# One 128x128 transpose for both heads' last 64 keys, with head 1's tail taken from its first 64 keys

## The chip, the core and the metric

The kernel runs on one core of a Trainium2 chip. The time is that of one execution on the device in microseconds (us), from three runs. A trace of one profiled execution gives the start and duration of the instructions of each engine: PE (TensorE matmuls; PEld is its weight load), DVE (VectorE), ACT (ScalarE), POOL (GpSimd) and SP (SyncE, which here only starts DMAs).

## The reference

Three blocks are chained; `B, H, S, D = 4, 8, 576, 64`, so the model width is 512.

```python
scores = scale * np.matmul(q, k.transpose(0, 1, 3, 2))
thresh = np.max(scores, axis=-1, keepdims=True) - tau
scores = np.where(scores >= thresh, scores, -1000000000.0)
attn = softmax(scores)                       # written out in the reference
x = (attn @ v) laid out as [B, S, H * D]
u = x + np.real(fft(fft(x, axis=1), axis=2))
un = (u - mean) / sqrt(var + 1e-06)
x = u + np.maximum(un @ w_ch1, 0.0) @ w_ch2
gate = sigmoid(causal convolution of x with conv_w, 5 taps)
out = (gate * (x @ w_val)) @ w_out
```

## The kernel before

The program order of each engine is written by hand. Attention runs over 16 pairs of heads (four pairs make one batch `b`). A pair has 576 queries a head, cut into nine tiles of 128 rows: for each of four blocks of 128 queries one tile for head 0 and one for head 1 (`h` = 0, 1), and one tile `h == 2` with the last 64 queries of both heads. That makes 144 tiles, two in each step of the loop `for u in range(NT // 2 + 3)`.

A tile goes through these stages, which the atoms of the string `ORDER` place within a step: S, the scores (PE, L573, into one of two PSUM score buffers); M, the row maximum (DVE, L585); E, the exponential (ACT, L592); K, the mask that multiplies the exponential with the comparison, writes the row tile `p` and sums the row (DVE, L602), and by that frees the score buffer; R and N, the reciprocal (DVE, L699) and the multiplication by it (POOL, L609, "the norm"); T, four 128x128 transposes of the probabilities, four tiles later (PE, L643); U, their copy from PSUM to SBUF (ACT, L652). S of the next tiles follows K of these.

A row tile `p` is [128, 1152]: head 0's 576 probabilities of 128 queries beside head 1's. Of the 576 keys, 512 (`MAIN`) go through the T transposes. The remaining 64 (`TAIL`, the last 64 of each head) are transposed by the tail work `g_tail` (L618 to L630): the transposes at L623 have 64 columns each and give a 64x128 result, ACT copies them to `th` (L628), and the product with `v` (`g_pv`, L302 to L325) ends with a fifth term that uses `th` against the tail rows `vt` of `v`, the lower 64 partitions of both being zero. There are four `p` buffers for five row blocks of a pair; the mask that starts on a buffer waits until the tail transposes of the block that held it are done.

PE's other work (tails, the transposes of q and k, the Fourier matmuls at L242, the products with v at L318) waits in queues. At P1 and P2 of each step `fill` draws from them up to a budget of estimated nanoseconds (1250 and 1350); each tail transpose counts 121.0, a product with v `n * 2 / 2.4`. Evacuations of finished fill work stand on ACT before the exponentials of the step (atom F1) or behind them (F2). `advance_side` (atom A) carries out the folds, the loads of v (`load_v`) and the addition of the FFT halves on DVE, POOL and SP. Conversions of the MLP's weights (WD, WP, WA; DVE L96 to L102, POOL L106) are spread over the steps. Behind attention `mlp` interleaves its first chunk with the Fourier work of batch 3 and then runs the MLP, the gate and the output.

Of the kernel before, what the change touches and what calls it, by code (L numbers as in the profile page):

```python
# [11 lines left out]
F32 = mybir.dt.float32  # L12
# [3 lines left out]
AF = mybir.ActivationFunctionType  # L16
ALU = mybir.AluOpType
# [4 lines left out]
B, H, S, D = 4, 8, 576, 64  # L22
# [4 lines left out]
MAIN, TAIL = 512, 64  # L27
# [107 lines left out]
def attention_fft(tc, right, ps_f, a, u_d, dram, conv_w, hooks):  # L135
    nc = tc.nc
    PE, DVE, ACT, POOL, SP = nc.tensor, nc.vector, nc.scalar, nc.gpsimd, nc.sync
    left, right1 = ExitStack(), ExitStack()
    with ExitStack() as right2, ExitStack() as right2b, ExitStack() as right3, ExitStack() as right4, ExitStack() as scores, ExitStack() as turned:
        def pool(stack, name, bufs, side="right", **kw):  # L140
            return stack.enter_context(tc.tile_pool(name=name, bufs=bufs, side=side, **kw))
# [3 lines left out]
        const = pool(right1, "const", 1)  # L145
# [13 lines left out]
        ident = id_p.tile([128, 128], F32, name="ident")  # L159
# [7 lines left out]
        ACT.activation(atau, alpha, AF.Exp)  # L167

        vs = [(const.tile([128, 2, 4, D], F32, name=f"v{i}"), const.tile([128, 2, D], F32, name=f"vt{i}")) for i in range(2)]
        ths = [[const.tile([128, 2, n], F32, name=f"th{i}_{n}") for n in (256, 320)] for i in range(2)]  # L170
        for t in [vt for _, vt in vs] + ths[0] + ths[1]:
            DVE.memset(t[64:128], 0.0)
        aeh = dft.tile([128, 3, CE], F32R, name="aeh")
        ael = dft.tile([128, 3, CE], F32R, name="ael")

# [33 lines left out]
        def load_v(p):  # L209
            b, hs = p // NP, slice(2 * (p % NP), 2 * (p % NP) + 2)  # L210
            v, vt = vs[p % 2]
            for h in range(2):
                SP.dma_start(out=v[:, h], in_=a["v"][b, hs, 0:MAIN][h].rearrange("(t p) d -> p t d", p=128))
            SP.dma_start(out=vt[0:64], in_=a["v"][b, hs, MAIN:S].rearrange("h p d -> p h d"))

        def g_consts():
            for nm, shape in (("cd", [128, 4, CE]), ("sd", [128, 4, DM // 2]), ("cs", [97, 3, KE]), ("ss", [96, 3, KE])):
# [14 lines left out]
        def fill_tile():  # L232
            state["open"] += 1
            return ps_f.tile([128, 512], F32, tag="f", name="f")

        def done(first, *then):

            evacs.append((first, then))
            state["put"] += 1
# [47 lines left out]
        def g_prep_v(p):  # L287
            while p >= 2 and (p - 2, 1) not in pv_done:
                yield
            load_v(p)  # L290
            vready.add(p)
# [3 lines left out]
        def x_tile(p):  # L295
            if p not in xt:
                xt[p] = x_p.tile([128, S], F32, tag="xt", name="xt")
            return xt[p]
# [3 lines left out]
        def g_pv(p, c):  # L302

            yield lambda: p in vready and tails.get((p, c), 0) == 1 + c and (p < XB or p - XB in folded)
            v, vt = vs[p % 2]
            x = x_tile(p)
            m, th = pt[p, c], ths[p % 2][c]
            yield "room"
            f = fill_tile()
            n = 256 if c == 0 else 320  # L310
            for t in range(5):
                for h in range(2):
                    w = v[:, h, t] if t < 4 else vt[:, h]
                    if t == 4:
                        r = th[:, h]
                    else:
                        r = m[:, h, t] if c == 0 else m[:, t, h * 320:h * 320 + 320]
                    PE.matmul(out=f[h * 64:h * 64 + 64, 0:n], lhsT=w, rhs=r, start=(t == 0), stop=(t == 4))  # L318
                    yield n * 2 / 2.4

            done(lambda: ACT.activation(x[:, c * 256:c * 256 + n], f[:, 0:n], AF.Copy))
            pv_done.add((p, c))
            if c == 1:
                yield "sync"
                side.append(g_fold(p))  # L325
# [5 lines left out]
        def g_fold(p):  # L331
            b, j = p // NP, p % NP
            x = xt.pop(p)
            while p and p - 1 not in folded or b and b - 1 not in spent_fold:
                yield
            if j == 0:
                fold[b] = [[fft_p.tile([128, NP, KE], F32R, tag=f"x{k}{i}", name=f"x{k}{i}") for i in "hl"] for k in "eo"]
                xs_d[b] = dram.tile([DM, S], F32, name=f"xs{b}")
            xs = xs_d[b]
            SP.dma_start(out=xs[j * 128:(j + 1) * 128], in_=x)  # L340
            xf = [None, None]
            w = (slice(0, HALF + 1), slice(1, HALF))

            def sums(kind):
                t = xf[kind] = tmp_p.tile([128, KE], F32, tag="xf", name="xf")
                POOL.tensor_tensor(out=t[:, 1:HALF], in0=x[:, 1:HALF], in1=x[:, S - 1:HALF:-1], op=ALU.subtract if kind else ALU.add)
                if kind == 0:
                    POOL.tensor_copy(t[:, 0:HALF + 1:HALF], x[:, 0:HALF + 1:HALF])  # L348

            def high_part(kind):  # L350
                ACT.activation(fold[b][kind][0][:, j, w[kind]], xf[kind][:, w[kind]], AF.Copy)

            def low_part(kind):
                h, l = (t[:, j, w[kind]] for t in fold[b][kind])
                POOL.tensor_tensor(out=l, in0=xf[kind][:, w[kind]], in1=f32(h), op=ALU.subtract)

            sums(0)
            yield
            sums(1)
            high_part(0)  # L360
            yield
            high_part(1)
            low_part(0)
            yield
            low_part(1)
            folded.add(p)
# [116 lines left out]
        q_prep, q_tail, q_pv, q_fft, q_mean = deque(), deque(), deque(), deque(), deque()  # L483
# [71 lines left out]
        p_t = {}  # L555

        def force(ready):
            while not ready():
                flush()
                advance_side()  # L560
                fill(1.0)
# [13 lines left out]

        def p_view(g):
            p, h, i = tiles[g]
            return p_t[p, i][:, h % 2 * S:h % 2 * S + S]

        def emit_max(g):  # L580
            if g % 2 == 0:
# [23 lines left out]
        def emit_norm(g):  # L605
            su = ssum[g // 2][:, g % 2:g % 2 + 1]
            v = p_view(g)
            p, h, i = tiles[g]
            POOL.tensor_scalar(out=v, in0=v, scalar1=su, scalar2=1.0, op0=ALU.mult, op1=ALU.mult)  # L609

        tq = []

        def pt_tile(p, c):
            if (p, c) not in pt:
                pt[p, c] = (pt0_p, pt1_p)[c].tile([128, 2, 4, 256] if c == 0 else [128, 4, 640], F32, tag=f"m{c}", name=f"m{c}")
            return pt[p, c]

        def g_tail(p, c, srcs, dst, rows):  # L618

            yield "room"  # L620
            f = fill_tile()
            for j, src in enumerate(srcs):
                PE.transpose(f[0:64, j * 128:(j + 1) * 128], src, ident)  # L623
                yield 121.0
            tailed.update((p, i) for i in rows)

            def first():
                ACT.activation(dst, f[0:64, 0:128 * len(srcs)].rearrange("k (h q) -> k h q", h=2), AF.Copy)  # L628
                tails[p, c] = tails.get((p, c), 0) + 1
            done(first)  # L630

# [2 lines left out]
        def emit_t(g):  # L634
            p, h, i = tiles[g]
            c = 0 if i < 2 else 1
            if (p, c) not in pt:
                force(lambda: p < 2 or (p - 2, c) in pv_done)
            m, th = pt_tile(p, c), ths[p % 2][c]
            f = ps_t.tile([128, 4, 128], F32, tag="t", name="t")  # L640
            pv = p_view(g)
            for t in range(4):
                PE.matmul(out=f[:, t, :], lhsT=pv[:, t * 128:(t + 1) * 128], rhs=ident, is_transpose=True, start=(t == 0), stop=(t == 3))  # L643
            if h == 2:
                o = m.rearrange("k t (h q) -> k t h q", h=2)[:, :, :, 256:320]
                fv = f.rearrange("k t (h q) -> k t h q", h=2)
            elif c == 0:
                o, fv = m[:, h, :, i * 128:(i + 1) * 128], f
            else:
                j = h * 320 + (i - 2) * 128  # L650
                o, fv = m[:, :, j:j + 128], f
            tq.append(lambda: ACT.activation(o, fv, AF.Copy))  # L652
            if h == 1 and i % 2 == 1:
                q_tail.append(g_tail(p, c, [p_t[p, i - 1 + j][:, hh * S + MAIN:hh * S + S] for hh in range(2) for j in range(2)], th[0:64, :, 0:256], (i - 1, i)))
            if h == 2:
                q_tail.append(g_tail(p, c, [p_t[p, i][:, MAIN:S]], th[0:64, :, 256:320], (i,)))

        LAG = 4
        SP.dma_start(out=ident, in_=a["ident"])
# [3 lines left out]
        for t in negs:  # L663
            for j in range(2):
                DVE.tensor_copy(t[:, j, 1:2], atau)
        DVE.tensor_scalar(out=alpha, in0=tau, scalar1=0.0, scalar2=float(D) ** -0.5,
                          op0=ALU.is_ge, op1=ALU.mult)
# [15 lines left out]
        for u in range(NT // 2 + 3):  # L683
            t = 2 * u
            on = [x for x in (t, t + 1) if x < NT]
            state["tile"] = t
            for x in on:
                p, h, i = tiles[x]
# [21 lines left out]
            def N0():  # L710
                if 0 <= t - 2 < NT: emit_norm(t - 2)
            def N1():
                if 0 <= t - 2 < NT: emit_norm(t - 1)
# [830 lines left out]
```

## Time and profile before

| what | value |
| --- | --- |
| times of three runs, us | 938.41, 938.17, 937.34 (median 938.17) |
| span of the profiled execution, first to last instruction, us | 936.0 (the page gives no other time of it) |
| busy share of PE, DVE, ACT, POOL | 94%, 59%, 48%, 39% |
| mean granted TensorE clock | 0.994 of full speed |
| steps of attention | from the start to about 395 us |
| one batch of attention (four pairs, 18 steps) | 96.5 us |

The busy shares are means over stages with different limits: the MLP keeps PE full, attention runs a loop over PE, DVE and ACT. What the change is worth has to be read in attention, where its instructions are, and at the places where other work waits for them.

### The profile page before, as it was taken

How to read it: one execution, taken by the hardware profiler on the slowest of the kernel's cores; microseconds unless marked ns; L12 is line 12 of the kernel's file. 1: busy time of each engine (PE TensorE's matmuls, PEld its weight loads, DVE VectorE, ACT ScalarE, POOL GpSimd, SP SyncE). 2: the span in 40 equal slices, each digit the busy share in tenths (PEclk: the TensorE clock that was granted, in tenths of full speed). 3: DMA queues.
4: the chain of work that ended last, by engine and by line, in shares of the span. 5: the costliest groups of instructions: out<-in, count | busy, mean ns of one | idle time of the engine just before them, and what ended most of it. 6: DMA issues, size and time to landing. Idle time of an engine off the chain costs nothing. (4 is left out here: it accounts for less than half of the span.)

```text
span 936.0 us, 14888 instructions
## 1 busy us (share of the span) xinstructions
PE 884.3 (94%) x5232; PEld 708.0 (76%) x5232; DVE 553.5 (59%) x1240; ACT 451.2 (48%) x915; POOL 368.0 (39%) x451
## 2 busy tenths in 40 slices
PE   6988899999999999799988999999999999999998
PEld 4555576657665765488866999999999989998897
DVE  5888888888887767316577243442412275735750
ACT  3778777777777766526355123213211313224432
POOL 2465645584467545612553321312111011037421
PEclk9999999999999999999999999999999999999999
DMA  6775545556555732587259524212110050233111
GB/s 151 190 193 129 165 119 167 154 163 173 164 142 172 193 92 72 178 314 234 89 204 351 204 91 130 79 46 85 52 66 1 1 178 3 91 130 122 70 46 68
DMA packets 135283, 123.34 MB, mean 132 GB/s; under 512 B 85686, under 2 KB 99238, under 8 KB 135208
## 3 DMA queue, kind: packets, MB, share of 16 engines
q1 hardware_dynamic: 126760, 97.57, 33.7%
q0 software_dynamic: 6960, 24.49, 8.5%
q8 instruction: 42, 0.69, 0.3%
q10 hardware_dynamic: 1488, 0.33, 0.2%
q14 instruction: 33, 0.27, 0.1%
HBM read 89.85 MB, written 37.22 MB: 136 GB/s over the span
## 5 line engine op out<-in xcount | busy, mean ns | idle before, releaser
L1072 DVE SCALAR_TENSOR_TENSOR hl<-h,hh 128x448 fp32r<-128x448 f32 (+1 forms) x80 | 51.0, 637 | 209.6 <-ACT hh L1071 209.6
L1071 ACT ACTIVATE hh<-h 128x448 fp32r<-128x448 f32 (+1 forms) x80 | 44.4, 555 | 262.9 <-PE h L1068 262.9
L609 POOL TENSOR_SCALAR p<-p,su 128x576 f32<-128x576 f32 x144 | 109.9, 769 | 91.1 <-DVE su L699 71.5
L602 DVE SCALAR_TENSOR_TENSOR p<-s,thr,e 128x576 f32<-128x576 f32 x144 | 112.6, 815 | 39.8 <-ACT e L592 21.9
L573 PE MATMUL s<-kt,qt 64*128 64x288 f32 (+1 forms) x640 | 101.3, 448 | 24.8 <-DVE p L602 24.8
L1084 PE MATMUL c<-hl,w1h 128*128 128x448 f32 (+1 forms) x320 | 118.9, 371 | 0.5 <-DVE hl L1072 0.5
L1084 PE MATMUL c<-hh,w1h 128*128 128x448 f32 (+1 forms) x320 | 118.8, 371 | 0.0
L1084 PE MATMUL c<-hh,w1l 128*128 128x448 f32 (+1 forms) x320 | 118.7, 371 | 0.0
L592 ACT ACTIVATE e<-s,neg 128x576 f32<-128x576 f32 x144 | 99.4, 737 | 28.5 <-DVE neg L585 27.9
L585 DVE TENSOR_REDUCE neg<-s 128x1 f32<-128x576 f32 x144 | 101.6, 745 | 14.5 <-PE s L573 14.5
L573 PEld LDWEIGHTS s<-kt,qt 64*128 64x128 f32 (+1 forms) x640 | 46.2, 178 | 66.3 <-issue 24.3
L652 ACT ACTIVATE m<-t 128x512 f32<-128x512 f32 x144 | 84.6, 588 | 6.5 <-PE t L643 6.4
L1068 PE MATMUL h<-unh,w0l 128*128 128x448 f32 (+1 forms) x320 | 81.9, 378 | 5.9 <-POOL w0l L106 5.9
L1068 PE MATMUL h<-unh,w0h 128*128 128x448 f32 (+1 forms) x320 | 80.5, 373 | 3.6 <-DMA w0h<-e_h 3.2
L318 PE MATMUL f<-m,v 128*64 128x320 f32 (+1 forms) x512 | 80.4, 415 | 1.5 <-ACT m L652 1.2
L1068 PE MATMUL h<-unl,w0h 128*128 128x448 f32 (+1 forms) x320 | 81.2, 376 | 0.0
L643 PE MATMUL t<-ident,p 128*128 128x128 f32 x576 | 77.9, 278 | 2.9 <-POOL xf L348 1.9
L643 PEld LDWEIGHTS t<-ident,p 128*128 128x128 f32 x576 | 64.3, 142 | 18.4 <-issue 10.3
L1068 PEld LDWEIGHTS h<-unh,w0l 128*128 128x128 f32 x320 | 60.8, 191 | 14.0 <-POOL w0l L106 7.2
L1068 PEld LDWEIGHTS h<-unh,w0h 128*128 128x128 f32 x320 | 59.9, 188 | 11.8 <-DMA w0h<-e_h 3.7
L1068 PEld LDWEIGHTS h<-unl,w0h 128*128 128x128 f32 x320 | 61.2, 191 | 7.2
L1084 PEld LDWEIGHTS c<-hl,w1h 128*128 128x128 f32 x320 | 60.1, 188 | 7.7 <-DVE hl L1072 0.9
(219 smaller groups left out, 1538.7 us busy)
## 6 DMA issues: line engine op xcount, KB each, us to landing
raw<-in_moe_w_ch POOLq DMA_DIRECT2D x32, 512.0 KB, 4.9
qn<-in_q SPq DMA_DIRECT2D x60, 128.0 KB, 2.9
xs<-xt SPq DMA_DIRECT2D x16, 288.0 KB, 4.1
e_h<-cx SPq DMA_DIRECT2D x18, 256.0 KB, 4.1
e_l<-ct SPq DMA_DIRECT2D x18, 256.0 KB, 5.3
w0h<-e_h SPq DMA_DIRECT2D x18, 256.0 KB, 6.7
w0l<-e_l SPq DMA_DIRECT2D x18, 256.0 KB
w1h<-e_h SPq DMA_DIRECT2D x18, 256.0 KB, 5.3
```

The source lines that it names most:

```text
L318: PE.matmul(out=f[h * 64:h * 64 + 64, 0:n], lhsT=w, rhs=r, start=(t == 0), stop=(t == 4))
L573: PE.matmul(out=s[o, c, 0:HALF], lhsT=qt[w, hh, q], rhs=kt[w, hh, :], start=True, stop=True)
L585: DVE.tensor_reduce(out=neg[i][:, j, 0:1], in_=sc[g][:, :, 0:HALF], axis=AX.XY, op=ALU.max, negate=True)
L592: ACT.activation(e, sc[g][:, :, 0:HALF], AF.Exp, bias=neg[g // 2][:, g % 2, 0:1], scale=1.0)
L602: DVE.scalar_tensor_tensor(out=p_view(g).rearrange("p (a b) -> p a b", a=2), in0=sc.pop(g)[:, :, 0:HALF], scalar=thr[g // 2][:, j], in1=ex ...
L609: POOL.tensor_scalar(out=v, in0=v, scalar1=su, scalar2=1.0, op0=ALU.mult, op1=ALU.mult)
L643: PE.matmul(out=f[:, t, :], lhsT=pv[:, t * 128:(t + 1) * 128], rhs=ident, is_transpose=True, start=(t == 0), stop=(t == 3))
L652: tq.append(lambda: ACT.activation(o, fv, AF.Copy))
L1068: PE.matmul(out=f[:, 0:n], lhsT=ww[:, k * 128:(k + 1) * 128], rhs=x[:, k, 0:n], start=(i == 0), stop=(i == 3 * KB - 1))
L1071: ACT.activation(hh, f[:, 0:n], AF.Relu)
L1072: DVE.scalar_tensor_tensor(out=hl, in0=f[:, 0:n], scalar=0.0, in1=f32(hh), op0=ALU.max, op1=ALU.subtract)
L1084: PE.matmul(out=ch[c][o][:, 0:n], lhsT=ww[:, o * 128:(o + 1) * 128], rhs=x, start=(at_ == 0 and i == 0), stop=(at_ == FB - 1 and i == 2))
```

## The change

Head 1's tail becomes its first 64 keys in place of its last 64. In a row of `p` head 0's last 64 columns (512 to 576) and head 1's first 64 (576 to 640) are neighbours, so one 128x128 transpose serves both heads. A pair then has five tail transposes of 128 columns (two for the first two row blocks, two for the next two, one for the tile `h == 2`) where it had nine of 64 columns; in all 80 and 144. `th` loses its head dimension; the zeros that keep the heads apart are now in `vt` alone, whose half for the other head is zero. The loads of v start 64 keys later for head 1, and the 64 rows for each head's `vt` come in two DMAs instead of one. In the tile `h == 2` both heads' queries share the columns of one mask, so the norm, which also puts them where the transposes expect them, becomes three POOL operations instead of one.

```diff
-        ths = [[const.tile([128, 2, n], F32, name=f"th{i}_{n}") for n in (256, 320)] for i in range(2)]
-        for t in [vt for _, vt in vs] + ths[0] + ths[1]:
-            DVE.memset(t[64:128], 0.0)
+        ths = [[const.tile([128, n], F32, name=f"th{i}_{n}") for n in (256, 320)] for i in range(2)]
+        for _, vt in vs:
+            for h in range(2):
+                DVE.memset(vt[64 - h * 64:128 - h * 64, h], 0.0)
...
             for h in range(2):
-                SP.dma_start(out=v[:, h], in_=a["v"][b, hs, 0:MAIN][h].rearrange("(t p) d -> p t d", p=128))
-            SP.dma_start(out=vt[0:64], in_=a["v"][b, hs, MAIN:S].rearrange("h p d -> p h d"))
+                src, o = a["v"][b, hs][h], h * TAIL
+                SP.dma_start(out=v[:, h], in_=src[o:o + MAIN].rearrange("(t p) d -> p t d", p=128))
+                o = (1 - h) * MAIN
+                SP.dma_start(out=vt[h * 64:h * 64 + 64, h], in_=src[o:o + TAIL])
...
                     if t == 4:
-                        r = th[:, h]
+                        r = th[:, 0:n]
...
-        return p_t[p, i][:, h % 2 * S:h % 2 * S + S]
+        return p_t[p, i][:, S if h else 0:S + S if h else S]
...
-            POOL.tensor_scalar(out=v, in0=v, scalar1=su, scalar2=1.0, op0=ALU.mult, op1=ALU.mult)
+            if h < 2:
+                parts = [(slice(0, 128), v, v)]
+            else:
+                rows = p_t[p, i]
+                parts = [(slice(0, 64), rows[:, 0:S], v), (slice(64, 128), rows[:, S:S + TAIL], v[:, 0:TAIL]),
+                         (slice(64, 128), rows[:, 0:MAIN], v[:, TAIL:S])]
+            for w, dst, src in parts:
+                POOL.tensor_scalar(out=dst[w], in0=src[w], scalar1=su[w], scalar2=1.0, op0=ALU.mult, op1=ALU.mult)
...
-            for j, src in enumerate(srcs):
-                PE.transpose(f[0:64, j * 128:(j + 1) * 128], src, ident)
+            th = ths[p % 2][c]
+            for j, i in enumerate(rows):
+                PE.transpose(f[:, j * 128:(j + 1) * 128], p_t[p, i][:, MAIN:MAIN + 2 * TAIL], ident)
                 yield 121.0
...
-                ACT.activation(dst, f[0:64, 0:128 * len(srcs)].rearrange("k (h q) -> k h q", h=2), AF.Copy)
+                if len(rows) == 2:
+                    ACT.activation(th[:, 0:256], f[:, 0:256], AF.Copy)
+                else:
+                    for h in range(2):
+                        w = slice(h * 64, h * 64 + 64)
+                        ACT.activation(th[w, 256:320], f[w, w], AF.Copy)
...
-            pv = p_view(g)
+            pv = p_t[p, i][:, S + TAIL:] if h == 1 else p_t[p, i][:, 0:MAIN]
```

The budgets of `fill` are as before, and so is the estimate of 121.0 for a tail transpose: with fewer of them, other work is drawn earlier, and the order on PE changes from the first batch's Fourier work on. From the first MLP matmul on it is the same again.

PE in the third batch of attention, before: the stretch from one pair of S (first two rows) to the next (the last row); `s<-kt,qt` are the scores, `t<-ident,p` the T transposes, `f<-ident,p` tails, `f<-m` and `f<-th` products with v, `f<-ssl,boh` Fourier matmuls.

```order
L573 MATMUL s<-kt,qt 128x288 x2
L573 MATMUL s<-kt,qt 64x288 x4
L242 MATMUL f<-ssl,boh 128x290 x3
L318 MATMUL f<-m_3332,v_197 64x256 x5
L643 MATMUL t<-ident,p 128x128 x8
L318 MATMUL f<-m_3332,v_197 64x256 x3
L318 MATMUL f<-th_256_201,vt_198 64x256 x2
L623 MATMUL f<-ident,p 64x128 x4
L318 MATMUL f<-m_3449,v_197 64x320
L573 MATMUL s<-kt,qt 128x288 x4
```

After, the stretch between the same two pairs of S (line numbers are those of the changed kernel):

```order
L576 MATMUL s<-kt,qt 128x288 x2
L576 MATMUL s<-kt,qt 64x288 x4
L245 MATMUL f<-csh,ael 128x290 x2
L245 MATMUL f<-csl,aeh 128x290 x3
L245 MATMUL f<-ssh,boh 128x290 x3
L245 MATMUL f<-ssh,bol 128x290 x3
L659 MATMUL t<-ident,p 128x128 x8
L245 MATMUL f<-ssl,boh 128x290 x3
L634 MATMUL f<-ident,p 128x128 x2
L576 MATMUL s<-kt,qt 128x288 x4
```

The product with v that stood on both sides of T has gone to other stretches, Fourier matmuls have come in, and the four tail transposes ahead of the next S have become two.

POOL near the end of attention, before: from the second half of the last two-half addition (`xr`) over the last norms (`p<-p,su`) to the first preparation of the fold behind them (`xel`).

```order
L464 TENSOR_TENSOR xr<-xr,dd 128x287
L609 TENSOR_SCALAR p<-p,su 128x576
L346 TENSOR_TENSOR xf<-xt 128x287
L348 COPY xf<-xt 128x2
L609 TENSOR_SCALAR p<-p,su 128x576
L346 TENSOR_TENSOR xf<-xt 128x287
L609 TENSOR_SCALAR p<-p,su 128x576
L355 TENSOR_TENSOR xel<-xf,xeh 128x289
```

After, the same place:

```order
L467 TENSOR_TENSOR xr<-xr,dd 128x287
L619 TENSOR_SCALAR p<-p,su 128x576
L349 TENSOR_TENSOR xf<-xt 128x287
L351 COPY xf<-xt 128x2
L619 TENSOR_SCALAR p<-p,su 128x576
L349 TENSOR_TENSOR xf<-xt 128x287
L619 TENSOR_SCALAR p<-p,su 64x576
L619 TENSOR_SCALAR p<-p,su 64x64
L619 TENSOR_SCALAR p<-p,su 64x512
L358 TENSOR_TENSOR xel<-xf,xeh 128x289
```

The last tile's norm has two more operations; the rest stands as it did. The same three stand in the place of one in every pair.

SP near the end of attention, before: `u_d` and `ur` are the stores of the FFT addition, `v` and `vt` the loads of the last pair's values, `xd` the load on which the second half of that addition rests.

```order
L456 DMA u_d_59<-xd 128x576
L340 DMA xs_4731<-xt 128x576
L466 DMA ur_0_4797<-xr 128x576
L468 DMA u_d_59<-ur_0_4797 16x36
L370 DMA u_d_59<-ur_0_4797 2x127x288
L213 DMA v_199<-in_v 128x4x64 x2
L214 DMA vt_200<-in_v 64x2x64
L432 DMA xd<-xs_3484 128x576
```

After, the same place (one `xs` load has moved ahead of it):

```order
L459 DMA u_d_59<-xd 128x576
L215 DMA v_199<-in_v 128x4x64
L217 DMA vt_200<-in_v 64x64
L215 DMA v_199<-in_v 128x4x64
L217 DMA vt_200<-in_v 64x64
L469 DMA ur_0_4799<-xr 128x576
L471 DMA u_d_59<-ur_0_4799 16x36
L373 DMA u_d_59<-ur_0_4799 2x127x288
L435 DMA xd<-xs_3267 128x576
```

The loads of the values now stand ahead of the stores, and `xd` comes directly behind the store `u_d<-ur` of 2x127x288, as it does before the change in the earlier batches.

## Rows read from the trace of the kernel before

**Rows 1.** The page's first part: busy us (share of the span) and instructions of each engine.

```profile
PE 884.3 (94%) x5232; PEld 708.0 (76%) x5232; DVE 553.5 (59%) x1240; ACT 451.2 (48%) x915; POOL 368.0 (39%) x451
```

**Rows 2.** Windows: length, PE, PEld, DVE, ACT, POOL busy, clock, DMA share, GB/s.

```profile
216.84:313.37 96.53, 91.62 (x675) 61.97 (x674) 79.30 (x193) 71.33 (x154) 57.10 (x77) 1.00 0.57 165
505.55:936.00 430.45, 425.35 (x2180) 387.98 (x2180) 183.04 (x370) 119.40 (x225) 102.69 (x101) 1.00 0.26 88
```

**Rows 3.** Waits of PE, whole span: us in total, times, longest.

```profile
PE s L573 <- DVE p L602: 24.8, 28, 2.4
```

**Rows 4.** Timeline of PE, third batch, scores only: start, us, operation, idle before.

```profile
240.87 1.50 PE L573 MATMUL s<-kt,qt 64*128 64x288 f32 x8 [0.63 <-DVE p L602]
245.86 0.51 PE L573 MATMUL s<-kt,qt 64*128 64x288 f32 x2 [1.05 <-DVE p L602]
...
278.38 1.40 PE L573 MATMUL s<-kt,qt 64*128 64x288 f32 x12
285.45 1.24 PE L573 MATMUL s<-kt,qt 64*128 64x288 f32 x8
291.01 1.24 PE L573 MATMUL s<-kt,qt 64*128 64x288 f32 x8
295.49 1.49 PE L573 MATMUL s<-kt,qt 64*128 64x288 f32 x8 [0.87 <-DVE p L602]
...
306.83 1.40 PE L573 MATMUL s<-kt,qt 64*64 64x288 f32 x12
311.02 1.25 PE L573 MATMUL s<-kt,qt 64*128 64x288 f32 x6 [0.75 <-DVE p L602]
```

**Rows 5.** Timeline of PE's weight loads, third batch: start, us, operation, count.

```profile
258.93 0.36 PEld L623 LDWEIGHTS f<-ident,p 128*64 128x64 f32 x4 [0.38 <-issue]
259.29 0.90 PEld L643 LDWEIGHTS t<-ident,p 128*128 128x128 f32 x8
...
271.62 1.27 PEld L318 LDWEIGHTS f<-m,v 128*64 128x64 f32 x10 [0.17 <-issue]
...
273.38 0.79 PEld L573 LDWEIGHTS s<-kt,qt 64*128 64x128 f32 x8 [0.49 <-PE f L318]
```

**Rows 6.** Single lines of the kernel: count, ns min/median/max, first and last start, shapes.

```profile
L628 ACT ACTIVATE th<-f x48: 258/582/594, 27.6 to 391.5; 64x512 f32<-64x512 f32 x32, 64x128 f32<-64x128 f32 x16
L321 ACT ACTIVATE xt<-f x32: 374/404/438, 38.8 to 395.2; 128x256 f32<-128x256 f32 x16, 128x320 f32<-128x320 f32 x16
L609 POOL TENSOR_SCALAR p<-p,su x144: 734/745/1434, 15.2 to 388.4; 128x576 f32<-128x576 f32 x144
L348 POOL COPY xf<-xt x16: 187/187/188, 49.1 to 396.7; 128x2 f32<-128x2 f32 x16
```

**Rows 7.** One line of DVE as in rows 6, and DVE and POOL on the timeline.

```profile
L97 DVE TENSOR_SCALAR ct<-raw x40: 407/422/1823, 41.4 to 628.4; 128x512 int32<-128x512 int32 x40
...
272.51 1.82 DVE L97 TENSOR_SCALAR ct<-raw 128x512 int32<-128x512 int32 x1
272.59 1.46 POOL L609 TENSOR_SCALAR p<-p,su 128x576 f32<-128x576 f32 x2
```

**Rows 8.** The end of attention on the timeline, an earlier `xd` load, and that line's landing times.

```profile
277.60 1.83 SPq L432 DMA_DIRECT2D xd<-xs  x1
...
366.87 1.37 PE L573 MATMUL s<-kt,qt 64*128 64x288 f32 x8
367.19 0.61 SPq L370 DMA_DIRECT2D u_d<-ur  x1
373.31 0.59 SPq L432 DMA_DIRECT2D xd<-xs  x1
378.24 0.80 POOL L453 TENSOR_TENSOR xd<-xd,dd 128x289 f32<-128x289 f32 x1 [5.41 <-DMA xd<-xs]
398.35 1.31 PE L1068 MATMUL h<-unh,w0h 128*128 128x512 f32 x4 [3.18 <-DMA w0h<-e_h]
...
DMA to landing us min/median/max: 8.6/9.0/17.0
```

More of the change, by code (lines that the diff above doesn't have):

```diff
@@ L616, in pt_tile, with g_tail @@
             return pt[p, c]
-        def g_tail(p, c, srcs, dst, rows):
+        def g_tail(p, c, rows):
             yield "room"
             f = fill_tile()
-            for j, src in enumerate(srcs):
-                PE.transpose(f[0:64, j * 128:(j + 1) * 128], src, ident)
+            th = ths[p % 2][c]
+            for j, i in enumerate(rows):
+                PE.transpose(f[:, j * 128:(j + 1) * 128], p_t[p, i][:, MAIN:MAIN + 2 * TAIL], ident)
                 yield 121.0
@@ L638, in emit_t @@
                 force(lambda: p < 2 or (p - 2, c) in pv_done)
-            m, th = pt_tile(p, c), ths[p % 2][c]
+            m = pt_tile(p, c)
             f = ps_t.tile([128, 4, 128], F32, tag="t", name="t")
-            pv = p_view(g)
+            pv = p_t[p, i][:, S + TAIL:] if h == 1 else p_t[p, i][:, 0:MAIN]
             for t in range(4):
@@ L653, in emit_t @@
             if h == 1 and i % 2 == 1:
-                q_tail.append(g_tail(p, c, [p_t[p, i - 1 + j][:, hh * S + MAIN:hh * S + S] for hh in range(2) for j in range(2)], th[0:64, :, 0:256], (i - 1, i)))
+                q_tail.append(g_tail(p, c, (i - 1, i)))
             if h == 2:
-                q_tail.append(g_tail(p, c, [p_t[p, i][:, MAIN:S]], th[0:64, :, 256:320], (i,)))
+                q_tail.append(g_tail(p, c, (i,)))
         LAG = 4
```

## The prediction, made before the result was known

> **What bounds the kernel now.** I read the page's busy shares first. PE is busy for 884.3 of the span's 936.0 us [rows 1], so the first guess would be that each PE microsecond saved is a microsecond of time. The windows show where that guess holds. Behind attention, from 505.55 to the end, PE is busy for 425.35 of 430.45 us; nothing of the change lies there. In a batch of attention it is busy for 91.62 of 96.53 us, and these ends of matmuls are modelled, so what is idle is rather more. POOL has 57.10 us of work there and DVE 79.30 [rows 2]. The waits then say what PE waits for in attention: the scores waited for the mask 28 times out of 72 steps, 24.8 us in all [rows 3]. So the loop is S, maximum, exponential, mask, S again, with the other PE work laid into it: where a step holds much of that work, PE ends last; where it holds little, the mask does. The timeline shows both kinds. From 278.38 to 285.45 is 7.07 us without a wait ahead of the second S; from 306.83 to 311.02 it is 4.19, from 291.01 to 295.49 4.48 and from 240.87 to 245.86 4.99 us, each with a wait for the mask [rows 4]. A saving on PE counts in the first kind of stretch and not in the others, and the reader should keep these three lengths in mind as the price of a stretch with little in it.
>
> **The change part by part.** *Tail transposes.* Four tail transposes of 64 columns have their weight loads done in 0.36 us, 0.09 each, with T right behind them; eight of 128 columns take 0.90 us, 0.113 each [rows 5]. A pair has two sets of four that become two of two: 0.36 − 2 × 0.113 = 0.135 saved twice, and its single one costs 0.023 more. That is 0.25 us a pair and 3.9 us over 16 pairs, if PE sets the end everywhere. The matmuls with `th` and `vt` keep their sizes.
>
> At this place the Trainium skill, page "TensorE: Matmul & The Clock Gate", Part 4 on the PE-mode transpose, gives some 275 ns for one 128x128 transpose inside a kernel. By that figure 64 fewer transposes would give an estimated 17.6 us. The weight loads of this trace follow one another at 0.09 us [rows 5], so the latency of one is not its price here, and the sum goes by the pitch.
>
> *The order of the fill.* The budgets stay, each removed transpose gives its 121 ns of budget to other work, and that work moves. The two stretches shown of the order are an example. Before, it holds S (0.79), three Fourier matmuls, 11 steps of products with v (two weight loads each, at most 0.127 by the 1.27 for 10), T (0.90) and a set of tails (0.36) [rows 5]. The Fourier matmuls, of 290 columns, I price like those of 320, at 0.127. With the pauses of 0.17 to 0.49 that the same rows show between kinds of work I count 6.9 us, and it took 7.07. After, the same stretch holds 14 Fourier matmuls, T and two tails, 4.2 us by the same count. I counted all stretches of the loop so. A batch of 18 holds 88.3 us before and 87.6 after; over the first 67 stretches it is 2.5 us less, not 3.9, because the new order changes kinds more often. But five stretches of a batch were shorter than 4.48 us, and nine are now: 4.13, 4.27, 3.96, 3.32, 4.32, 3.34, 4.17, 3.12 and 2.79. In these the mask ends last. If each stretch takes the larger of its content and 4.19 us, the 67 stretches shrink by 0.7; with 4.48 they grow by 1.7; with 4.99 by 5.4 [rows 4]. I take the middle of the first two, as two of the three short stretches of [rows 4] lie there: +0.5.
>
> *A wait that goes.* The stretch of 4.99 us has five tail transposes ahead of its S, and its mask could write its buffer only behind them; no stretch of the new order has more than three tails there. I give it 4.99 − 4.48 = 0.5 in each of 2.6 batches (67 stretches less the first 20, by 18): −1.3. Its bounds are 0 and that. Attention thus changes by −0.8.
>
> *ACT.* 32 copies of 64x512 at 0.58 us become 128x256, for which the nearest row has 0.37 to 0.44; 16 copies of 64x128 at 0.26 become two of 64x64, at most 0.26 each [rows 6]. At 0.18 saved 32 times, less at most 0.26 given back 16 times, ACT gains some 2 us. It counts for nothing: ACT is busy for 71.33 of 96.53 us [rows 2]. Where the copy stands ahead of an exponential, the exponential starts up to 0.2 earlier; this lies inside the bounds of the stretch lengths.
>
> *POOL.* The norm of the tile `h == 2` was one 128x576 operation of 0.745 us. Between that and the 128x2 copy at 0.187 lie 574 columns, 0.97 ns each [rows 6]; the first of the three parts keeps 576 columns and so 0.745, the others have 64 and 512: 0.25 + 0.68 = 0.93 us more, 14.9 in all. No row shows a 64-partition operation on POOL; if half the partitions took half the time, it would be 0.1 instead of 0.93. I cost it at nothing: POOL has 96.53 − 57.10 = 39 us free in a batch against 3.7 added [rows 2], and T needs the norm only two steps later. With that cover gone it is the slower rival below.
>
> *DVE, SP, memory.* Four memsets go, at the start, ahead of the first scores and behind loads that are still on their way: 0. The second DMA for each `vt`, 16 in all, is on SP, which waits for nothing that PE needs except at the end of attention: 0 within it.
>
> *The end of attention.* First comes the chain from `xd`: it is issued at 373.31, lands for POOL at 378.24, and the first MLP matmul starts at 398.35, 20.1 us behind it. Before, the loads of v hold `xd` back; after, it comes directly behind the store that starts at 367.19 and lasts 0.61. Landing took 4.9 us here, but the line's median is 9.0 [rows 8]. So the early bound is 367.8 + 0.4 + 9.0 = 377.2, 1.0 before 378.24. In the earlier batch, where `xd` also comes directly behind that store, it was issued at 277.60, 4.2 us behind the S of 273.38 [rows 5, 8]; from the S of 366.87 that and 9.0 give 380.1, 1.9 late. The middle is +0.4, which I take.
>
> **The sum.** −0.8 in attention, +0.4 at its end: −0.4. The span of 936.0 becomes 935.6; it lies 2.2 below the median of the runs, 938.17, and with that the forecast is 937.8 us. A difference of 0.2%, 1.9 us, is about what a measurement of this kernel can tell from none, so I forecast no change.
>
> **The rivals.** *Faster.* The PE work saved counts everywhere and the short stretches get quicker, since fewer tails stand ahead of the mask: −2.5 for the content, −1.3 for the wait that goes, −1.0 at `xd`. That is −4.8, or 933.4. For it speaks that 44 of 72 steps had no wait for the mask [rows 3]; against it, that there are four more short stretches in a batch.
>
> *Slower, by the split norm.* On the timeline a DVE operation whose median is 0.42 us took 1.82, from 272.51, while two norms ran on POOL from 272.59 for 1.46 us [rows 7]. DVE's maximum, mask and weight conversions share a queue, so a conversion held by the two added norms holds the mask behind it, and in a short stretch S waits for that mask. Of 16 × 0.93 = 14.9 us, a third on the path would give +5 and 943; it is slower than 0.2% from 2.3 us on, 16% of the time added. Against it: mean busy times of POOL leave room, and only a conversion standing beside the norm pays.
>
> The Trainium skill speaks for this rival, on the page "SBUF — State Buffer", section "Who interferes with whom": DVE in a two-port mode and GpSimd share a pair of ports under an exclusive lock that lasts the whole instruction, and the loser blocks fully. The trace agrees, with the 1.82 beside 0.42 just named [rows 7].
>
> *Nothing moves.* Tails and fill are both hidden behind the mask, as in the short stretches: 938.2, no change too, and counted with the forecast.
>
> **How the numbers follow.** No change, from 936.3 to 940.0, has 0.40; faster 0.33; slower 0.27, most of it the split norm, the rest stretches at 4.99 us (+5.4) or a late `xd`. The range reaches to both rivals: 933.4 and 943.0.
>
> **What the changed profile would show.** Tail weight loads 128 columns wide at 0.11 to 0.12 each, two to a set. About as many waits of the scores for the mask as before, perhaps more, in shorter lengths; if the forecast is right a batch is within 1 us of 96.5. POOL's norm of 64x512 at about 0.68. `xd` landing 11 to 13.5 us behind the S it belongs to, where before it was 378.24 − 366.87 = 11.4 [rows 8]. I am wrong on the fast side if the batch falls below 95.5, by PE's content or by shorter loops; on the slow side if DVE operations beside the split norm are long and the scores' wait for the mask grows by several us over 24.8.

## The result, and the profile after

The changed kernel takes 950.16 us (median of four runs, 947.36 to 952.34); the kernel before takes 938.06. The ratio is 1.0128, with a 95% interval of 1.0107 to 1.0149: 12.1 us slower, well outside the predicted 933.4 to 943.0. A trace shows one execution, for the changed kernel the longest of its four (952.34 us, mean clock 0.984) and for `order_only` and `one_norm` below the shortest of their five (943.42 and 945.74, both at 0.993), so lengths of stretches in different kernels are not set against each other to the microsecond.

The page's first part for the changed kernel, as in [rows 1]:

```profile
PE 891.0 (94%) x5168; PEld 704.9 (74%) x5168; DVE 554.5 (58%) x1238; ACT 451.1 (47%) x931; POOL 381.2 (40%) x483
```

64 matmul instructions are gone and PE is busy for 6.7 us more: a first sign that some of its work ran at a lower clock. A stretch, here and below, is the time from one S to the next. Windows of the changed kernel: a batch, and then two stretches from S to S at the end of the second batch and two at the end of the third (columns as in [rows 2]).

```profile
218.44:321.00 102.56, 94.72 (x658) 61.66 (x657) 78.44 (x192) 71.80 (x158) 60.64 (x84) 0.97 0.52 152
```
```profile
194.67:204.15 9.48, 4.41 (x26) 3.05 (x25) 3.49 (x10) 4.74 (x10) 6.20 (x10) 0.79 0.58 179
204.15:213.43 9.28, 9.28 (x46) 5.19 (x47) 6.06 (x15) 5.66 (x14) 7.28 (x10) 0.66 0.26 80
298.91:306.87 7.96, 3.63 (x27) 2.44 (x26) 3.49 (x10) 4.19 (x8) 5.64 (x10) 0.94 0.52 180
306.87:315.99 9.12, 9.12 (x46) 5.12 (x47) 6.03 (x15) 6.27 (x15) 7.74 (x10) 0.67 0.25 73
```

The batch takes 102.6 us where it took 96.5 [rows 2]. The same two stretches of the third batch, 291.01 to 295.49 and on to 301.12 in the kernel before, took 10.1 us; they take 17.1 now. The two pairs hold 15.6 us more than before, so that all other stretches together are some 3 us shorter: last S at 390.13 against 377.58, 12.5 us later. In the first stretch of each pair PE is idle for more than half of the time, in the second it is busy throughout, at a granted clock of 0.66 to 0.67.

Waits of PE, DVE and POOL in the changed kernel (us in total, times, longest):

```profile
PE s L576 <- DVE p L605: 25.2, 34, 2.5
...
DVE p L605 <- PE f L634: 14.9, 9, 5.9
...
PE t L659 <- POOL p L619: 13.3, 9, 2.6
```
```profile
POOL xd L456 <- DMA xd<-xs: 11.1, 2, 7.7
POOL xd L456 <- DMA v<-in_v: 4.4, 1, 4.4
```

The scores wait for the mask about as long as in [rows 3]. What has grown is a chain of three: POOL waits for `xd` (in the kernel before only at the end of attention), T for the norm on POOL (0.9 us in all before), the mask for the tails on PE (9.0 us in 5 waits before, the longest 2.7). The wait of 7.7 us is that at the end of attention. One of the three waits of POOL is put down to a load of v; its `xd` load too had been issued only some 8 us before (189.94, POOL's addition at 197.73), so I read it as the same.

Timeline of SP, then of all engines, at the end of the third batch in the changed kernel (start, us, engine, line, operation):

```profile
284.88 0.45 SPq L215 DMA_DIRECT2D v<-in_v  x1
...
287.26 0.54 SPq L469 DMA_DIRECT2D ur<-xr  x1
289.57 0.54 SPq L471 DMA_DIRECT2D u_d<-ur  x1
290.17 0.66 SPq L373 DMA_DIRECT2D u_d<-ur  x1
290.93 2.06 SPq L343 DMA_DIRECT2D xs<-xt  x1
293.04 0.42 SPq L435 DMA_DIRECT2D xd<-xs  x1
```
```profile
301.01 0.79 POOL L456 TENSOR_TENSOR xd<-xd,dd 128x289 f32<-128x289 f32 x1 [3.41 <-DMA xd<-xs]
301.79 0.73 POOL L619 TENSOR_SCALAR p<-p,su 128x576 f32<-128x576 f32 x1
...
302.58 0.66 PE L659 MATMUL t<-ident,p 128*128 128x128 f32 x4 [1.68 <-POOL p L619]
303.17 1.79 POOL L619 TENSOR_SCALAR p<-p,su 64x576 f32<-64x576 f32 x3
...
305.02 0.66 PE L659 MATMUL t<-ident,p 128*128 128x128 f32 x4 [1.78 <-POOL p L619]
...
305.51 0.49 PE L634 MATMUL f<-ident,p 128*128 128x128 f32 x3
...
305.99 0.82 DVE L605 SCALAR_TENSOR_TENSOR p<-s,thr,e 128x576 f32<-128x576 f32 x1 [4.36 <-PE f L634]
...
306.87 2.29 PE L576 MATMUL s<-kt,qt 64*128 64x288 f32 x8 [0.87 <-DVE p L605]
```

Read it from the top. The store `ur` could go from 282.68, when POOL was done with it, but stands behind loads of q, v and `vt` and starts at 287.26; two more stores and the store `xs` later `xd` is issued at 293.04. (`xs<-xt` writes attention's output to memory; the remark under the SP order above calls it a load.) POOL is at its addition by 297.6 and waits 3.41 us. The norms stand behind that addition on POOL's queue, and one of them is the split one (1.79 us for its three parts). T waits for each, the tails stand behind T, the mask needs the row buffer that the tails free, and S needs the mask. Then S takes 2.29 us where it took 1.24 [rows 4], at a granted clock of 0.5. In the order before, `xd` was issued at 277.60 [rows 8] for an addition at 289.55, and nothing waited.

### The profile page after: what moved, and what is told of

The parts are those of the page before. It is cut to its first block, busy times and chain, and to the rows that moved or that the text cites. A ratio compares the mean times of both kernels' runs of the same rounds, so it can differ in the third digit from the quotient of the medians.

```text
span 950.6 us, 14815 instructions
## 1 busy us (share of the span) xinstructions
PE 891.0 (94%) x5168; PEld 704.9 (74%) x5168; DVE 554.5 (58%) x1238; ACT 451.1 (47%) x931; POOL 381.2 (40%) x483
## 5 line engine op out<-in xcount | busy, mean ns | idle before, releaser
L619 POOL TENSOR_SCALAR p<-p,su 128x576 f32<-128x576 f32 (+3 forms) x176 | 124.5, 714 | 70.8 <-DVE su L715 59.2
L576 PE MATMUL s<-kt,qt 64*128 64x288 f32 (+1 forms) x640 | 103.5, 453 | 25.3 <-DVE p L605 25.2
L659 PE MATMUL t<-ident,p 128*128 128x128 f32 x576 | 79.6, 280 | 13.3 <-POOL p L619 13.3
L321 PE MATMUL f<-m,v 128*64 128x320 f32 (+1 forms) x512 | 84.8, 435 | 1.3 <-ACT m L668 1.3
```

The costliest lines, as they stand in the source:

```text
L576: PE.matmul(out=s[o, c, 0:HALF], lhsT=qt[w, hh, q], rhs=kt[w, hh, :], start=True, stop=True)
L619: POOL.tensor_scalar(out=dst[w], in0=src[w], scalar1=su[w], scalar2=1.0, op0=ALU.mult, op1=ALU.mult)
```

## The experiments

Twelve runs in three groups of four; each group shares the runs of the kernel before, with medians of 936.88, 936.39 and 936.48 us. Ratios are to those, with 95% intervals.

**The order alone, the change without it.** Two kernels: the change with the budget that gives PE's old order, and the old operations in the new order.

```diff
 budget (from the changed kernel):
-                yield 121.0
+                yield 121.0 * len(rows)
 order_only (from the kernel before):
-                yield 121.0
+                if len(srcs) == 1 or j % 2:
+                    yield 121.0
```

> The changed kernel with one edit: each transpose of a set of two counts 242 ns of the fill budget instead of 121, so that a set costs the budget what the four did. With it PE's order is that of the kernel before again, with the new tails in the old places. Order theory (the moved fill makes the load of xd for the second half of the FFT addition late, POOL waits for it with norms behind, T, tails, mask and scores follow late, and PE's clock falls): 933 to 938 us, no stretch from S to S above 8 us in the batches, no wait of POOL for xd above 1 us before the end of attention. Norm theory (the split norm costs the time): 946 to 951, as the changed kernel.

> The kernel before with one edit: a set of four tail transposes counts 242 ns of the fill budget instead of 484. PE's order is then that of the changed kernel, but with four tails of 64 columns, one norm and one vt load as before. Order theory: 947 to 953 us, with the long stretches (about 9 us each, two in a row, at the end of the second and of the third batch) and POOL's wait for xd ahead of them. Norm theory: 936 to 941, since the split norm is not there. If the two loads of vt instead of one are what makes xd late, 940 to 945.

Measured: `budget` 936.09 us, ratio 0.9994 (0.9981 to 1.0006); `order_only` 947.33, 1.0103 (1.0083 to 1.0123). The change without its new order costs nothing that can be measured, and the new order without the change costs 1.0%. The two `vt` loads are not needed for it. POOL's addition at the end of the third batch in `budget`, without a wait:

```profile
288.52 0.82 POOL L456 TENSOR_TENSOR xd<-xd,dd 128x289 f32<-128x289 f32 x1
```

and the chain in `order_only`, with one norm of 0.74 in the place of three:

```profile
294.95 0.79 POOL L453 TENSOR_TENSOR xd<-xd,dd 128x289 f32<-128x289 f32 x1 [3.38 <-DMA xd<-xs]
...
299.85 0.82 DVE L602 SCALAR_TENSOR_TENSOR p<-s,thr,e 128x576 f32<-128x576 f32 x1 [4.26 <-PE f L623]
...
300.74 2.29 PE L573 MATMUL s<-kt,qt 64*128 64x288 f32 x8 [0.66 <-DVE p L602]
```

Long stretches at both places were expected, and the profiled execution has them in the third batch only (7.9 us each). At the second batch's end POOL waited 2.57 us, T 0.83 and 0.72, the clock stayed at 1.00, and the two stretches took 6.3 and 6.6.

**POOL's wait as the link: the addition a step later.**

```diff
+            if j == 1 and b < B - 1:
+                yield
+                yield
             POOL.tensor_tensor(out=x[:, up], in0=x[:, up], in1=dd[:, up], op=ALU.add)
```

> The changed kernel with the second half of the FFT addition (POOL's first operation on xd and all behind it) begun one step later, in batches 0 to 2. Nothing else moves. Order theory, with POOL's wait for xd as the link: the two pairs of 9 us stretches become some 5 to 6 us each, 935 to 941 us in all; the wait of DVE's mask for tails falls from 14.9 us to below 8. If instead the order hurts by late tails or in another way than through POOL's wait, the time stays at 947 to 953. Norm theory: 948 to 952.

Measured: 944.13 us, 1.0079 (1.0063 to 1.0096), between the two cases. The two pairs of long stretches did go, to 4.5 and 6.6 us each, and the mask's wait for tails fell from 14.9 to 6.0. But a new stretch of 10.8 us appeared earlier in the third batch, where the changed kernel has 7.4. Its timeline in `late_add`:

```profile
224.39 0.64 SPq L373 DMA_DIRECT2D xr<-xs  x1
225.13 9.68 SPq L952 DMA_DIRECT2D e_h<-cx  x1
...
241.69 0.43 DVE L96 TENSOR_SCALAR cx<-raw 128x512 int32<-128x512 int32 x1 [5.28 <-DMA e_h<-cx]
...
245.00 1.33 PE L579 MATMUL s<-kt,qt 64*128 64x288 f32 x4 [4.01 <-DVE p L608]
```

A weight conversion on DVE waits for its buffer `cx`, whose store `e_h` stands on SP behind another that, behind the copy `xr<-xs`, could not be issued for 9.68 us; maximum and mask stand behind the conversion. So the moved order has a second place where SP's queue is late, and the new delay brought it out.

**The clock as a cost of its own.**

```diff
+            if g in (70, 71, 106, 107):
+                for t in range(16):
+                    PE.matmul(out=f[:, t % 4, :], lhsT=ident, rhs=ident, start=True, stop=True)
```

> The changed kernel with 16 added matmuls of 128x128 (identity by identity, into the PSUM tile that the transposes then overwrite) ahead of the transposes of four tiles, those that wait for the norms in the two long places. It adds about 2 us of PE work ahead of each of the four, in time in which PE sat idle. If the fall of the granted clock is a cost of its own, the stretch behind each stall shrinks from 9.1 to some 6 us and the time falls to 943 to 947; if the clock is only a sign of the stall, 949 to 955.

Measured: 950.5 us, 1.0149 (1.0131 to 1.0167): no gain, as was expected for a clock that is only a sign. The stretches say otherwise. The windows of the second batch's pair, to be set against the first two of the four above:

```profile
195.46:206.66 11.20, 10.34 (x90) 9.62 (x89) 3.49 (x10) 5.35 (x12) 8.53 (x14) 1.00 0.46 158
206.66:213.23 6.57, 6.57 (x47) 3.70 (x47) 5.72 (x15) 5.02 (x11) 3.26 (x5) 1.00 0.28 70
```

The stretch behind the stall fell from 9.28 to 6.57 us with the clock at 1.00, and at the third batch's end from 9.12 to 6.56, so the low clock costs 2.7 and 2.6 us. `late_add`, without added matmuls, takes the same 6.57 and 6.56 there, also at 1.00. The time did not show it, since 16 added matmuls took 3.7 us and not the 2 that I had reckoned, and lengthened the stalls by 1.7 and 3.25 us. The prices are separate; the trade is about even.

**SP's queue as the first link: `xd` loaded early.** `early_xd` is the changed kernel, `early_xd_budget` the same in the old order.

```diff
             SP.dma_start(out=u_d[b][j * 128:(j + 1) * 128], in_=x)
+            if j == 0 and b < B - 1:
+                ahead[b] = fft_p.tile([128, S], F32, tag="xd", name="xd")
+                SP.dma_start(out=ahead[b], in_=xs[128:256])
             yield
```

> The changed kernel with the load of xd for the second half of the FFT addition issued in batches 0 to 2 right behind the store that frees its buffer, ahead of the loads of v and vt and of the stores that it stood behind; xr is loaded where it was. Order theory, now with SP's queue as the first link: POOL's wait for xd in the batches goes (it was 4.4 and 3.4 us), the two pairs of long stretches (18.8 and 17.1 us) come down to some 11 to 13, and the time to 934 to 940. If the norms behind POOL's wait were late for another reason, the long stretches stay and the time is 947 to 952. A wait of DVE for the weight store e_h, as it came with the later addition, would show as 941 to 945.

> The kernel with the old budget (PE's order as before) and the early load of xd of the run above. In that order POOL did not wait for xd in the batches, so both theories expect no change from the same order without it: 934 to 938 us. A saving of more than 2 us would mean that xd was late in a way that the waits do not show.

Measured: `early_xd` 940.53 us, 1.0055 (1.0036 to 1.0073), a little above its range. Against the kernel before of its own group it is 4.1 us slower where the change was 12.1: 8.0 us come back by moving one load in three batches. The kernel before gains 2.2 us by the same load (`early_before`, below), so some 6 of the 8 are the waits within attention. POOL waits for no `xd` any more, and the first stretch of each pair is 4.8 us. Three long stretches are left (columns as above):

```profile
199.37:207.52 8.15, 8.15 (x47) 4.38 (x47) 6.00 (x14) 6.16 (x15) 7.12 (x11) 0.79 0.28 100
237.13:245.74 8.61, 6.56 (x44) 3.86 (x43) 5.28 (x14) 3.50 (x8) 4.08 (x6) 1.00 0.50 178
315.95:323.17 7.22, 7.22 (x46) 5.13 (x45) 4.37 (x11) 5.55 (x13) 3.15 (x5) 0.76 0.70 186
```

The first and the last are busy throughout at a low clock, the last just behind a wait of PE of 1.85 us for the load `tn`; in the middle one DVE waits 3.10 us for `e_h`. `early_xd_budget` 934.24, 0.9978 (0.9962 to 0.9995): a gain at the end of attention, where POOL's wait of 5.4 us for `xd` [rows 8] is gone; its expectation had left that place out. With the same early load the new order is still 6.3 us slower than the old one, so the late `xd` is about half of what the order costs.

**The split norm, taken out of the change and put into the kernel before.**

```diff
 one_norm (from the changed kernel):
-            if h < 2:
+            if True:
 split_norm (from the kernel before):
+                parts = [(slice(0, 64), v), (slice(64, 128), v[:, 0:TAIL]), (slice(64, 128), v[:, TAIL:S])]
```

> The changed kernel with the norm of the tile h == 2 as one 128x576 operation in place; the part of the computation that moves head 1's probabilities of that tile to their places is left out. If the split norm only adds its 1.05 us where POOL is already late (two places, with what follows at a lower clock), 944 to 948. If it is the cause, 936 to 940. If it costs nothing at all, 949 to 951.

> The kernel before with the norm of the tile h == 2 in three operations of 64x576, 64x64 and 64x512, in place; all else as before. Order theory: hidden in POOL's idle time, 935.5 to 938. Norm theory: 942 or more; half of 14.9 us would show as 944.

Measured: `one_norm` 947.74 us, 1.0132 (1.0105 to 1.0159), the same ratio as the change's; `split_norm` 939.07, 1.0030 (1.0016 to 1.0044), 2.7 us. So the split norm is not the cause, but by its median it isn't free either. In the old order T waits more for norms, 6.0 us where it was 0.9, 3.8 of it at the end of attention:

```profile
PE t L648 <- POOL p L614: 6.0, 8, 1.4
```

Yet the first MLP matmul starts no later for it (398.26 us, before 398.35), so where the 2.7 us arise is not shown. In the profiled execution of `one_norm` the two pairs take 13.3 and 12.6 us at a clock of 1.00, some 10 us less than the change's together; DVE's wait for `e_h` takes 3.5 back (9.2 and 7.0 us in the stretches where the change has 7.4 and 5.4). Its other four executions were up to 4.1 us longer, and no trace shows their stretches. Groups of the norm in the changed kernel by shape (count | busy us, mean ns | idle before):

```profile
L619 POOL TENSOR_SCALAR p<-p,su 128x576 f32<-128x576 f32 x128 | 95.7, 752 | 55.4 <-DVE su L715 52.4 <-PE s L576 2.2
...
L619 POOL TENSOR_SCALAR p<-p,su 64x576 f32<-64x576 f32 x16 | 12.4, 778 | 14.2 <-DVE su L715 6.8 <-PE f L280 4.2 <-PE s L576 3.2
...
L619 POOL TENSOR_SCALAR p<-p,su 64x512 f32<-64x512 f32 x16 | 11.2, 700 | 0.0
...
L619 POOL TENSOR_SCALAR p<-p,su 64x64 f32<-64x64 f32 x16 | 5.8, 360 | 1.2
```

**Both loads early, and whose gain it is.** `early_both` adds the same for `xr`, behind its own store; `early_before` is the kernel before with the early `xd` alone; `early_xd_budget2` repeats a run beside it.

```diff
             SP.dma_start(out=rev, in_=xr)
+            if j == 0 and b < B - 1:
+                t = ahead[b, "xr"] = fft_p.tile([128, S], F32, tag="xr", name="xr")
+                SP.dma_start(out=t, in_=rv[128:256])
```

> The changed kernel with both loads for the second half of the FFT addition issued as soon as their buffers are free, xd behind its store and xr behind its own, in batches 0 to 2. With xd alone the time was 940.5 us, POOL then waited for xr and the stretches behind were 8.15 and 7.22 us. Order theory: the wait for xr shrinks and so do those stretches, to 935 to 939 us; what is left over the kernel before is the wait of DVE for the store e_h (a stretch of 8.6 where its content is 6.7) and the split norm. If the time stays at 940 to 942, xr was not what ended last.

> The same two early loads with the old budget (PE's order as before). POOL's wait for xr at the end of attention was 2.8 us with the early xd alone, so up to 2 us less than that run: 932 to 935. No gain on it would mean that w0h, the first MLP weight, is what ends last there.

> The kernel before, without any of the change, with the early load of xd alone. If the gain of the old budget with the early xd comes from the end of attention, where POOL waited 5.4 us for xd, this kernel has it too: 934 to 936. If it comes from the change's fewer transposes, this one stays at 936 to 938.

> The changed kernel with the old budget and the early load of xd again, on the chip of the other three, so that it can be set against the kernel before with the same early load. Expected 933 to 936, and within 1 us of the kernel before with the early load, since the split norm's price and the fewer transposes about cancel.

Measured: `early_both` 940.55 us, 1.0047 (1.0032 to 1.0062), no further gain: the pairs are down to 4.8 and 6.6, but the stretch with the wait for `e_h` (4.26 us now) is 9.8. `early_both_budget` 933.4, 0.9968 (0.9955 to 0.9981), the fastest of all, and 7.15 us faster than `early_both`, which differs from it by the order alone. `early_before` 934.32, 0.9972 (0.9959 to 0.9985), and `early_xd_budget2` 934.64, 0.9973 (0.9961 to 0.9986): equal. The gain over the kernel before is thus that of the early load; the change itself is worth nothing that shows, in either company.

## Why the prediction was wrong

**The step that failed** is the one on SP: that it "waits for nothing that PE needs except at the end of attention: 0 within it". I had seen that `xd` hangs on what stands before it in SP's queue, and priced that only at the end of attention, where the trace of before already showed a wait. (The slower rival names a late `xd` too, as a rest without a price.) The moved order puts loads of q, k and v and the store `xs` ahead of it in each batch. `order_only` and `budget` show that the order is the cause: new order without the change 1.0103, change without the new order 0.9994. `early_xd` shows what the late `xd` is worth: some 6 us within attention, about half. In what remains the traces show DVE waiting for `e_h`, another transfer that SP issues late; that this wait is the other half is argued from its length, not shown.

**The stretches.** I let each take the larger of its PE content and the loop's shortest length, and let nothing else be late. Where nothing is, that holds: `late_add` has 4.5 and 6.6 us in the places of the long pairs, and the change's other stretches lost some 3 us together, against my −0.8. What the count could not see is a step whose T waits for POOL.

**A wait that goes.** This term, −1.3, rests on a misreading. In the stretch of 4.99 us the tails had ended at 244.81 us, and what ended the mask's wait was the exponential:

```profile
244.98 0.82 DVE L602 SCALAR_TENSOR_TENSOR p<-s,thr,e 128x576 f32<-128x576 f32 x1 [0.86 <-ACT e L592]
```

The steps that took 4.98 or 4.99 us in the second, third and fourth batch take 5.12, 5.37 and 5.12 in the changed kernel: nothing went.

**Tail transposes.** Their saving was priced too low. The set with weight loads done in 0.36 us [rows 5] takes 0.46 on PE, from its start at 258.94 to T's at 259.40, and by the starts in both traces tails of 64 columns (before) and of 128 (`budget`) follow one another at the same median of 0.109 us. PE is busy for 90.20 us in the 96.53 us window of [rows 2] in `budget`, against 91.62 there before, and over the whole span for 5.3 us less where I had 3.9:

```profile
PE 879.0 (94%) x5168; PEld 702.2 (75%) x5168; DVE 550.4 (59%) x1238; ACT 449.3 (48%) x931; POOL 384.0 (41%) x483
```

The time does not show it. That kernel also carries the split norm, for which `split_norm` shows 2.7 us, and comes out equal, so the saving may be about as large; no run has it by itself.

**POOL.** The added time was 0.70 + 0.36 + 0.78 − 0.75 = 1.09 us a tile, against my 0.93; the 64x64 part was mis-sized most, 0.36 for 0.25. Calling it hidden was wrong by 2.7 us in the old order, by the median. That T needs the norm only two steps later was no cover where POOL itself was late: in the changed kernel T waits for it at each long place. As a rival the split norm had the right sign in the old order, neither the size nor the way. DVE was not held by it: of 54 weight conversions on DVE within attention (L96, L97 and L102) 12 take over 0.5 us in the kernel before, each beside a POOL operation, 12 in `split_norm` and 5 in the changed kernel. Nor did the sign for the slow side show, since the scores' wait for the mask is 25.2 us against 24.8. What the split norm adds at the two long places is not settled: 1.09 us of work each, some 5 us each by the profiled execution of `one_norm`, nothing by its ratio.

**The end of attention.** `xd` came 9.0 us behind its issue, as the line's median had said, and from the last S to the first MLP matmul it took 21.2 us against 20.8: +0.5, where I had +0.4. The rest of the span behind it is 1.6 us longer (539.2 us for 537.6). It lies between 536.4 and 539.2 in all the traces, and is 537.1 in `early_xd` in the same order, so I don't put it down to the change.

**What stays open.** Of the 7.15 us by which `early_both` is still slower than `early_both_budget`, its stretches of 9.8 and 7.0 us with DVE's wait for `e_h`, 4.8 and 5.0 in the old order, explain the most by their length; no run took that wait alone away.

## What to carry to other kernels

When a change frees budget in a hand-made schedule, the work that moves takes its DMA issues along: list, for each load that an in-order engine waits for, what now stands ahead of it in its queue, in every repetition of the pattern and not only where the trace already shows a wait. The quickest test is to hold the order and change the operations, and the reverse; here two short edits told the cause. A queue with slack by its mean can still hold the work that ends last, so try issuing a load as soon as its buffer is free; here one such load gained 0.2 to 0.3% in the old order.

## What the runs showed of the hardware

Two waits of PE of 1.7 and 1.8 us, close together (302.58 and 305.02 in the changed kernel), were followed by some 7 us at half the granted clock: eight score matmuls took 2.29 us for 1.24, and the stretch 9.12 us against 6.56 in `late_add` and `busy_pe`, 2.6 us lost on top of the wait itself. SP could not issue the next store for 9.7 us behind a copy of 255 rows in reversed order (225.13 in `late_add`); the kernel before has such a place too, 9.3 us long (124.35), without anything waiting on it. Transposes of 64 and of 128 columns followed one another on PE at the same median of 0.109 us. And a POOL operation of 64x64 took 0.36 us, where a line through 128x576 and 128x2 gives 0.25.
